# Linear attention and a GELU layer on one core: longer idle products at the start, and another order of chunk 3 and the state products

## The chip, the cores and the metric

The kernel runs on one core of one Trainium2 chip. The metric is the device time of one execution in microseconds (us), as the median of several runs. A profile is one further execution, recorded by the hardware profiler; its span runs from the first to the last instruction.

## The reference

Decayed linear attention over 4 batches, 8 heads, 768 positions and a head size of 64, block by block, and then two matrix products with an exact GELU between them, on all 3072 tokens:

```python
intra = einsum('bhic,bhjc->bhij', qb, kb) * Dmask      # lam ** (i - j) for i >= j, else 0
intra = einsum('bhij,bhjd->bhid', intra, vb)
inter = einsum('bhid,bhde->bhie', qb * lam_pow, kv_state)
out[block] = intra + inter
kv_state = lam_block * kv_state + einsum('bhsd,bhse->bhde', kb * rev_pow, vb)
...
x = out.transpose(0, 2, 1, 3).reshape(3072, 512)
result = gelu(x @ w_in) @ w_out                        # 512 -> 2048 -> 512
```

All inputs and the result are float32 in device memory.

## The kernel before

The kernel works in chunks of 128 positions of one batch, with all heads: 24 chunks, numbered so that four of them (one per batch, the same 128 positions) form a group of 512 tokens. There are six groups. A chunk goes through these steps, each a function of the kernel:

- `transposed`: the matrix engine (TensorE, PE in the profile) transposes keys and queries through PSUM (L169), and another engine copies them out (kT and qT, L172).
- `scores`: products of kT and qT into two PSUM banks (L196); `masked` multiplies them by the decay mask on VectorE (DVE, L204).
- `outputs`: the masked scores times v (L231), for later groups also the queries times the state (L226); the result is copied into x_t (L239 on ScalarE, ACT, for the first groups), the input of the MLP.
- `next_state`: keys times decayed values (v_dec, made by `decay_v`, L163, on GpSimd, POOL) into a PSUM bank with the tag "t", of which there is one (L211). VectorE empties it into the state (L215), which the chunk of the same batch in the next group needs.

The MLP of a group (`mlp_blocks`) is a list of blocks: the first layer, with its GELU on ScalarE (h_ps, L412, into g_t, L416), and the second layer. For group 0 the first layer has 21 blocks, cut so that the first of them need only the first chunks of x_t: blocks 0 to 5 use chunks 0 and 1, blocks 6 and 7 chunk 2, blocks 8 to 13 chunks 0 to 2, blocks 14 to 16 chunk 3, and blocks 17 to 20 all four. The second layer of group 0 is in plain form (L426); later groups use seven products of half blocks in place of eight.

The order of all work is written out by hand. Each engine takes its instructions in the order of the program, and a wait for another engine holds up what stands behind it. Three parts fix the order:

- The opening, straight-line code from `make_powers()` on. `keep_warm(n)` puts n idle products (L470) with a zero operand into PE's stream; `new=False` uses the PSUM bank of the last such run.
- `group0`, a table from the number of a block of group 0 to the steps that are issued just before that block.
- `todo`, a sorted list for all later groups.

Loads are issued by GpSimd in one queue: for chunks 0 to 3 the keys, queries and values with the pieces of w_in between them, then v_dec of chunks 0 to 2, two quarters of w_out, v_dec of chunk 3, two more quarters, and the loads of chunk 4 and so on.

PSUM is tight: the tags "sc", "mh" and "mo" have two banks each, "t" and "o" one. `transposed` takes "mh" for keys and "mo" for queries; each block of the first layer takes "mh"; idle products and the second layer take "mo".

Of the kernel before, what the change touches and what calls it, by code (L numbers as in the profile page):

```python
# [15 lines left out]
def kernel(  # L16
# [123 lines left out]
    def make_lam_blk():  # L140
        for hi in range(2):
            p = slice(hi * D, (hi + 1) * D)
            nc.scalar.copy(lam_blk[p, :, p], lam_c_b[p])
# [7 lines left out]
    def bank(shape, dtype, tag, name):  # L151
        return ps.tile(shape, dtype, tag=tag, name=name, bufs=2 if tag in ("sc", "mh", "mo") else 1)
# [12 lines left out]
    def transposed(c, name, tag, empty):  # L165

        src, t_ps = getattr(c, name), bank([128, HP, C], BF16, tag, "t_ps")
        for hp in range(HP):
            nc.tensor.transpose(t_ps[:, hp, :], src[:, 2 * hp:2 * hp + 2, :], ident)  # L169
        dst = work_pool.tile([128, HP, C], BF16, tag=name + "T", name=name + "T")  # L170
        setattr(c, name + "T", dst)
        empty(dst, t_ps)  # L172
# [18 lines left out]
    def scores(c):  # L191
        sc_ps = [bank([128, HP, C], F32, "sc", f"sc_ps{hi}") for hi in range(2)]
        for hp in range(HP):
            for hi in range(2):
                p = slice(hi * D, (hi + 1) * D)
                nc.tensor.matmul(sc_ps[hi][:, hp, :], c.kT[p, hp, :], c.qT[p, hp, :], start=True, stop=True)  # L196
        c.sc_m = work_pool.tile([128, HP, 2, C], BF16, tag="sc_m", name="sc_m")
        c.sc_ps = sc_ps
        for hi in range(0 if c.n == 0 else 2):
            masked(c, hi)  # L200

    def masked(c, hi):
        mask = decay[:, hi] if c.early else cmask[:, None, :].to_broadcast((128, HP, C))
        nc.vector.tensor_mul(c.sc_m[:, :, hi, :], c.sc_ps[hi], mask)  # L204

    def next_state(c):
        if c.sb == NB - 1:
            return
        kv_ps = bank([128, HP, 128], F32, "t", "kv_ps")
        for hp in range(HP):  # L210
            nc.tensor.matmul(kv_ps[:, hp, :], c.k[:, 2 * hp:2 * hp + 2, :], c.v_dec[:, 2 * hp:2 * hp + 2, :],  # L211
                             start=True, stop=True)
        new = work_pool.tile([128, HP, 128], BF16, tag="state_f", name="state", bufs=8)
        if c.sb == 0:
            nc.vector.tensor_mul(new, kv_ps, lam_blk)  # L215
        else:
            tmp = work_pool.tile([128, HP, 128], F32, tag="tmp", name="tmp")
            nc.vector.tensor_add(tmp, kv_ps, states[c.n])  # L218
            nc.vector.tensor_mul(new, tmp, lam_blk)  # L219
        states[c.n + M] = new  # L220

    def outputs(c, x_t, off, evacuate=True):
        o_ps = bank([128, HP, C], F32, "o", "o_ps")
        if c.sb > 0:
            for hp in range(HP):
                nc.tensor.matmul(o_ps[:, hp, :], states[c.n][:, hp, :], c.qT[:, hp, :],  # L226
                                 start=(hp == 0), stop=False, skip_group_check=True)
        v = c.v if c.early else c.v_dec
        for hi in range(2):
            for hp in range(HP):  # L230
                nc.tensor.matmul(o_ps[hi * D:(hi + 1) * D, hp, :], v[:, 2 * hp + hi, :], c.sc_m[:, hp, hi, :],  # L231
                                 start=(c.sb == 0 and hp == 0), stop=True, skip_group_check=True)
        c.x_o, c.o_ps = x_t[:, :, off * C:(off + 1) * C], o_ps
        if evacuate:
            empty_outputs(c)
# [225 lines left out]
    live = {}  # L461
# [3 lines left out]
    def keep_warm(n, new=True, cols=256):  # L465

        if new:
            idle_ps[0] = bank([128, 512], F32, "mo", "idle_ps")
        for _ in range(n):
            nc.tensor.matmul(idle_ps[0][:, :cols], idle[:, :128], idle[:, :cols], start=True, stop=True)  # L470

    def early(n):
        live[n] = begin(n, early=True)
        return live[n]
# [3 lines left out]
    def causal(hi):  # L478
        nc.vector.tensor_mul(decay[:, hi], decay[:, hi], cmask[:, None, :].to_broadcast((128, HP, C)))

    make_powers()
    nc.scalar.activation(warm, pos, ACT.Gelu)
    keep_warm(8, cols=512)
    c = early(0)
    causal(0)
    transposed(c, "k", "mh", copy)
    keep_warm(1, new=False)
    transposed(c, "q", "mo", copy)
    causal(1)
    keep_warm(1)  # L490
    scores(c)
    for hi in range(2):
        masked(c, hi)
# [6 lines left out]
    nc.scalar.copy(w_in_t[:, :, :256], wide_w)  # L500
    keep_warm(2)
    scores(c)
    keep_warm(8, new=False)
    make_lam_blk()
    outputs(live[1], xT[0], 1)
    c = early(2)
# [34 lines left out]
    def both_transposed(c):  # L541
        transposed(c, "k", "mh", nc.vector.tensor_copy)
        transposed(c, "q", "mo", nc.vector.tensor_copy)
# [2 lines left out]
    group0 = {  # L546
        1: [lambda: scores(live[2])],
        5: [lambda: outputs(live[2], xT[0], 2)],
        9: [lambda: both_transposed(live[3])],
        10: [lambda: scores(live[3]), lambda: next_state(live[0])],  # L550
        11: [lambda: next_state(live[1])],
        12: [lambda: outputs(live[3], xT[0], 3)],
        13: [lambda: next_state(live[2])],
        17: [lambda: next_state(live[3])],
        e: [w_out_sums, lambda: decay_v(live[4], nc.vector)],
        e + 8: [lambda: transposes(live[4])],
# [79 lines left out]
```

## Time and profile before

| | |
|---|---|
| median of 3 runs | 211.65 us (211.26 to 211.77) |
| profiled execution | 211.83 us |
| its span | 210.1 us |
| PE busy | 201.6 us (96%) |
| VectorE busy | 139.1 us (66%) |
| ScalarE busy | 81.6 us (39%) |
| GpSimd busy | 96.0 us (46%) |

Busy times are sums over the whole span. PE's matrix products are pipelined: the length of a row holds the passage through the array, so successive rows overlap, and a row's count times the distance of two starts is the better measure of work. In the rows of the order of time, the first number is the start in us from the beginning of the span, the second the length; "x8" is the number of instructions merged into the row; what stands in brackets is the idle time of the engine just before it and what ended that.

### The profile page before, as it was taken

The numbers are of one execution on the slowest core, as the hardware profiler recorded it, in microseconds if no ns is written. First come the engines' busy times: TensorE is split into PE (matmuls) and PEld (weight loads), VectorE is DVE, ScalarE is ACT, GpSimd is POOL, SyncE is SP. The second block draws the span as 40 slices with busy tenths as digits, with TensorE's granted clock in tenths as the row PEclk, the third lists the DMA queues.
The fourth block names the chain that finished last, engine by engine and source line by source line (L and its number), as shares of the span: only waits on it lengthen the run. The fifth ranks groups of instructions, "written<-read, shape, count | busy, mean of one in ns | idle before, by whom it ended". The sixth has DMA issues, their size and how long they took to land.

```text
span 210.1 us, 4145 instructions
## 1 busy us (share of the span) xinstructions
PE 201.6 (96%) x1718; PEld 131.1 (62%) x1718; DVE 139.1 (66%) x220; ACT 81.6 (39%) x145; POOL 96.0 (46%) x112
## 2 busy tenths in 40 slices
PE   6799799999999999999999999999999999999992
PEld 1567484556544688655688655688655688544881
DVE  4742529455568869698779688579778579223482
ACT  5856264132565420155520255420265420366200
POOL 8999953999999990299500394000100000000000
PEclk9999999999999999999999999999999999999999
DMA  5999999999999999499990599110552000500014
GB/s 117 153 174 177 200 207 186 155 216 151 146 223 144 157 165 98 158 158 150 162 77 0 188 142 172 33 21 3 204 107 41 3 0 3 200 0 0 3 50 150
DMA packets 102370, 24.65 MB, mean 117 GB/s; under 512 B 92880, under 2 KB 99536, under 8 KB 102352
## 3 DMA queue, kind: packets, MB, share of 16 engines
q0 software_dynamic: 80688, 13.37, 88.2%
q1 hardware_dynamic: 21664, 11.02, 23.2%
q8 instruction: 13, 0.21, 0.4%
q14 instruction: 5, 0.04, 0.1%
HBM read 27.27 MB, written 6.29 MB: 160 GB/s over the span
## 4 chain that ended last, share of the span: by engine, by line
PE 92%; DMA 2%; DVE 1%; ACT 1%; POOL 1%; issue 1%; POOLq 0%
PE h_ps L412 40%; PE r_ps L306 9%; PE p_ps L306 8%; PE q_ps L306 8%; PE o_ps L426 7%; PE o_ps L231 4%; PE s_ps L306 4%; PE sc_ps L196 4%; DMA q_t<-in_q_dram 2%; PE o_ps L226 2%; PE kv_ps L211 2%; PE t_ps L169 2%; PE idle_ps L470 1%; ACT g_t L416 1%; POOL k_t L67 0%
## 5 line engine op out<-in xcount | busy, mean ns | idle before, releaser
L412 PE MATMUL h_ps<-x_t,w_in_t 128*128 128x512 bf16 (+3 forms) x460 | 90.0, 344 | 0.6 <-ACT g_t L416 0.2
L416 ACT ACTIVATE g_t<-h_ps 128x512 bf16<-128x512 f32 (+2 forms) x101 | 58.1, 576 | 81.6 <-PE h_ps L412 81.3
L412 PEld LDWEIGHTS <-w_in_t 128*128 128x128 bf16 x460 | 40.1, 98 | 36.6 <-issue 1.5
L163 POOL TENSOR_TENSOR v_dec<-v_t,lam_m 128x512 bf16<-128x512 bf16 x23 | 24.5, 1079 | 48.1 <-PE kv_ps L211 47.0
L306 PEld LDWEIGHTS <-g_sum 128*128 128x128 bf16 x400 | 38.5, 98 | 5.1
L281 DVE TENSOR_TENSOR g_sum<-g_t 128x1024 bf16<-128x1024 bf16 x50 | 33.4, 716 | 10.7 <-ACT g_t L416 10.7
L204 DVE TENSOR_TENSOR sc_m<-sc_ps,cmask 128x512 bf16<-128x512 f32 x40 | 25.6, 682 | 2.0 <-PE sc_ps L196 2.0
L67 POOL DMA_DIRECT2D k_t<-in_k_dram x24 | 22.1, 922 | 2.2 <-DMA w_out_t<-in_moe_w_out_dram 2.0
L67 POOL DMA_DIRECT2D q_t<-in_q_dram x24 | 21.5, 898 | 2.3 <-DMA w_out_t<-in_moe_w_out_dram 2.3
L67 POOL DMA_DIRECT2D v_t<-in_v_dram x24 | 21.4, 893 | 2.0 <-DMA w_out_t<-in_moe_w_out_dram 1.7
L306 PE MATMUL r_ps<-w_sum,g_sum 128*128 128x256 bf16 x160 | 19.3, 273 | 0.0
L241 DVE TENSOR_TENSOR x_t<-o_ps,lam_q 128x512 bf16<-128x512 f32 x16 | 11.0, 688 | 10.2 <-PE o_ps L231 10.2
L306 PEld LDWEIGHTS <-g_t 128*128 128x128 bf16 x160 | 15.3, 98 | 3.2
L218 DVE TENSOR_TENSOR tmp<-kv_ps,state 128x512 f32<-128x512 f32 x16 | 11.0, 690 | 7.4 <-PE kv_ps L211 7.4
L426 PE MATMUL o_ps<-w_out_t,g_t 128*128 128x512 bf16 x64 | 15.3, 380 | 0.0
L219 DVE TENSOR_TENSOR state<-tmp,lam_blk 128x512 bf16<-128x512 f32 x16 | 14.8, 923 | 0.5
L196 PE MATMUL sc_ps<-qT,kT 64*128 64x128 bf16 x192 | 10.0, 226 | 0.3 <-DVE qT L172 0.3
L306 PE MATMUL p_ps<-w_sum,g_t 128*128 128x256 bf16 x80 | 10.1, 273 | 0.0
L306 PE MATMUL q_ps<-w_sum,g_t 128*128 128x256 bf16 x80 | 9.7, 273 | 0.0
L426 PEld LDWEIGHTS <-g_t 128*128 128x128 bf16 x64 | 5.8, 98 | 6.1
L306 PE MATMUL q_ps<-w_out_t,g_sum 128*128 128x256 bf16 x80 | 9.6, 273 | 0.0
L306 PE MATMUL s_ps<-w_sum,g_sum 128*128 128x256 bf16 x80 | 9.6, 273 | 0.0
(65 smaller groups left out, 168.1 us busy)
## 6 DMA issues: line engine op xcount, KB each, us to landing
out_dram<-o_sb SPq DMA_DIRECT2D x9, 512.0 KB, 3.0
k_t<-in_k_dram POOLq DMA_DIRECT2D x24, 128.0 KB, 6.0
q_t<-in_q_dram POOLq DMA_DIRECT2D x24, 128.0 KB, 6.2
v_t<-in_v_dram POOLq DMA_DIRECT2D x24, 128.0 KB, 6.5
w_out_t<-in_moe_w_out_dram POOLq DMA_DIRECT2D x4, 512.0 KB, 10.4
w_in_t<-in_moe_w_in_dram POOLq DMA_DIRECT2D x7, 256.0 KB, 7.9
out_dram<-o_sb SPq DMA_DIRECT2D x5, 256.0 KB, 5.2
wide_w<-in_moe_w_in_dram SPq DMA_DIRECT2D x1, 512.0 KB, 4.1
```

Of the source, the lines that this page charges most:

```text
L67: nc.gpsimd.dma_start(raw[n, name], chunk_of(name, n))
L163: eng.tensor_mul(c.v_dec, c.v, lam_m[:, :, None].to_broadcast((128, H, D)))
L196: nc.tensor.matmul(sc_ps[hi][:, hp, :], c.kT[p, hp, :], c.qT[p, hp, :], start=True, stop=True)
L204: nc.vector.tensor_mul(c.sc_m[:, :, hi, :], c.sc_ps[hi], mask)
L218: nc.vector.tensor_add(tmp, kv_ps, states[c.n])
L219: nc.vector.tensor_mul(new, tmp, lam_blk)
L241: nc.vector.tensor_mul(c.x_o, c.o_ps, lam_q)
L281: nc.vector.tensor_tensor(gsum[i][:, ks, :], g_t[:, ka + k:ka + k + n4, ta], g_t[:, kb + k:kb + k + n4, tb], op=op)
L306: nc.tensor.matmul(o, left[i](k, slice(u * C, (u + 1) * C)), right[i](k), start=(begin and k == 0), stop=(k == KH - 1), skip_group_check=True)
L412: nc.tensor.matmul(h_ps[:, k, lo:hi], w_in_t[:, ki, (kf + k) * 128:(kf + k + 1) * 128], x_t[:, ki, cols.start + lo:cols.start + hi], start ...
L416: nc.scalar.activation(g_t[:, kf:kf + ks, cols], h_ps, ACT.Gelu)
L426: nc.tensor.matmul(om[io], g_t[:, kf, io * C:(io + 1) * C], w_out_t[:, kf, :], start=(kf == 0), stop=(kf == NK2 - 1))
```

## The change

In the opening, the first run of idle products goes from eight to eleven of 512 columns; behind the transposes of chunk 0's keys stand three idle products of 256 columns in place of one, behind those of its queries two in place of one, and before the outputs of chunk 1 nine in place of eight.

In the table for group 0, the state products of chunks 0, 1 and 2 move from ahead of blocks 10, 11 and 13 to ahead of blocks 6, 7 and 9. The transposes of chunk 3 move from ahead of block 9 to ahead of block 8. The scores of chunk 3 stay ahead of block 10, its outputs ahead of block 12, and the state product of chunk 3 ahead of block 17.

```diff
     make_powers()
     nc.scalar.activation(warm, pos, ACT.Gelu)
-    keep_warm(8, cols=512)
+    keep_warm(11, cols=512)
     c = early(0)
     causal(0)
     transposed(c, "k", "mh", copy)
-    keep_warm(1, new=False)
+    keep_warm(3, new=False)
     transposed(c, "q", "mo", copy)
     causal(1)
-    keep_warm(1)
+    keep_warm(2)
     scores(c)
...
     scores(c)
-    keep_warm(8, new=False)
+    keep_warm(9, new=False)
     make_lam_blk()
     outputs(live[1], xT[0], 1)
...
     group0 = {
         1: [lambda: scores(live[2])],
         5: [lambda: outputs(live[2], xT[0], 2)],
-        9: [lambda: both_transposed(live[3])],
-        10: [lambda: scores(live[3]), lambda: next_state(live[0])],
-        11: [lambda: next_state(live[1])],
+        6: [lambda: next_state(live[0])],
+        7: [lambda: next_state(live[1])],
+        8: [lambda: both_transposed(live[3])],
+        9: [lambda: next_state(live[2])],
+        10: [lambda: scores(live[3])],
         12: [lambda: outputs(live[3], xT[0], 3)],
-        13: [lambda: next_state(live[2])],
         17: [lambda: next_state(live[3])],
```

## The prediction

> **What bounds the kernel now.** I read the page's head first, then the waits of the matmul engine (PE), then the order of time, for PE and for the engines that feed it.
>
> ```profile
> span 210.1 us, 4145 instructions
> ...
> PE 201.6 (96%) x1718; PEld 131.1 (62%) x1718; DVE 139.1 (66%) x220; ACT 81.6 (39%) x145; POOL 96.0 (46%) x112
> ```
> ```profile
> PE t_ps L169 <- DMA k_t<-in_k_dram: 1.3, 1, 1.3
> ...
> PE kv_ps L211 <- DVE state L215: 1.0, 1, 1.0
> ...
> PE h_ps L412 <- ACT g_t L416: 0.2, 1, 0.2
> PE h_ps L412 <- ACT x_t L239: 0.2, 1, 0.2
> ```
>
> PE is busy for 96% of the span, and the second fence holds the waits of PE that matter (two of 0.3 stand in the rows below). So PE's own stream sets the end, and whatever moves the stream forward early moves the end, unless a transfer is late afterwards. But a busy PE is not one at full speed, which the opening shows in the order of time (start, length, what; x is a count):
>
> ```profile
> 1.19 3.59 PE L470 MATMUL idle_ps<-idle 128*128 128x512 bf16 x8 [1.19 <-DVE idle L101]
> ...
> 2.02 0.15 PEld L470 LDWEIGHTS <-idle 128*128 128x128 bf16 x1 [0.28 <-issue]
> ...
> 3.73 0.15 PEld L470 LDWEIGHTS <-idle 128*128 128x128 bf16 x1 [0.28 <-issue]
> ...
> 6.12 0.61 PE L169 MATMUL t_ps<-ident,k_t 128*128 128x128 bf16 x4 [1.34 <-DMA k_t<-in_k_dram]
> 6.53 0.42 PE L470 MATMUL idle_ps<-idle 128*128 128x256 bf16 x1
> 7.22 0.61 PE L169 MATMUL t_ps<-ident,q_t 128*128 128x128 bf16 x4 [0.27 <-DMA q_t<-in_q_dram]
> ...
> 8.34 0.61 PE L196 MATMUL sc_ps<-qT,kT 64*128 64x128 bf16 x8 [0.30 <-DVE qT L172]
> ...
> 10.35 0.63 PE L169 MATMUL t_ps<-ident,q_t 128*128 128x128 bf16 x4
> ...
> 12.58 1.29 PE L470 MATMUL idle_ps<-idle 128*128 128x256 bf16 x8
> ...
> 14.34 0.40 PE L169 MATMUL t_ps<-ident,k_t 128*128 128x128 bf16 x4
> ...
> 15.07 0.60 PE L412 MATMUL h_ps<-x_t,w_in_t 128*128 128x256 bf16 x4
> ```
>
> Four transposes take 0.61 to 0.63 us up to 10.35 and 0.40 at 14.34. Eight idle products of 256 columns fit into 1.29 us at 12.58, where the single one at 6.53 took 0.42. So PE ran at half rate until about 13.1, inside the idle run at 12.58. The first idle run of 3.59 us did not raise the rate; unbroken work from 8.34 to 13.1, 4.8 us, did. In between lie the waits of 1.34, 0.27 and 0.30.
>
> The second place is the stage of chunk 3 and the state products:
>
> ```profile
> 17.22 3.13 POOL L163 TENSOR_TENSOR v_dec<-v_t,lam_m 128x512 bf16<-128x512 bf16 x3
> ...
> 18.34 0.61 PE L412 MATMUL h_ps<-x_t,w_in_t 128*128 128x256 bf16 x4
> 18.46 0.59 ACT L239 CAST x_t<-o_ps 128x512 bf16<-128x512 f32 x1
> ...
> 19.10 1.50 PE L412 MATMUL h_ps<-x_t,w_in_t 128*128 128x128 bf16 x24 [0.15 <-ACT x_t L239]
> ...
> 20.19 0.87 ACT L416 ACTIVATE g_t<-h_ps 128x512 bf16<-128x512 f32 x2 [0.82 <-PE h_ps L412]
> ...
> 20.84 0.81 PE L412 MATMUL h_ps<-x_t,w_in_t 128*128 128x384 bf16 x4 [0.24 <-ACT g_t L416]
> 21.48 0.39 PE L169 MATMUL t_ps<-ident,k_t 128*128 128x128 bf16 x4
> ...
> 22.25 0.41 DVE L172 COPY qT<-t_ps 128x512 bf16<-128x512 bf16 x1
> 22.97 0.40 PE L196 MATMUL sc_ps<-qT,kT 64*128 64x128 bf16 x8
> 23.30 0.40 PE L211 MATMUL kv_ps<-v_dec,k_t 128*128 128x128 bf16 x4
> 23.40 1.29 DVE L204 TENSOR_TENSOR sc_m<-sc_ps,decay 128x512 bf16<-128x512 f32 x2 [0.73 <-PE sc_ps L196]
> 23.53 0.81 PE L412 MATMUL h_ps<-x_t,w_in_t 128*128 128x384 bf16 x4
> 24.61 0.68 DVE L215 TENSOR_TENSOR state<-kv_ps,lam_blk 128x512 bf16<-128x512 f32 x1
> 25.34 0.40 PE L211 MATMUL kv_ps<-v_dec,k_t 128*128 128x128 bf16 x4 [1.00 <-DVE state L215]
> 26.32 0.42 PE L231 MATMUL o_ps<-sc_m,v_t 128*64 128x128 bf16 x8
> 26.68 0.82 PE L412 MATMUL h_ps<-x_t,w_in_t 128*128 128x384 bf16 x4
> ```
>
> The state product of chunk 1 (25.34) waits 1.00 us for its PSUM bank, tag "t", of which there is one. The vector engine empties it at 24.61, only after both masks of chunk 3 (23.40, 1.29 us). Two more waits fall on the activation engine: 0.24 us before block 8 for the Gelu of block 6, and 0.15 before block 6 for chunk 2's outputs.
>
> I count what PE issues by start to start, since lengths hold a tail of about 0.17 us. From the rows: a block of 4x384 is 0.64 (20.84 to 21.48), of 4x256 0.44 (0.61 less the tail), of 16x128 0.89 and of 8x128 0.45 (1.50 less 0.16, over 24); a state product 0.23, scores 0.33, outputs 0.36, one chunk's two transposes 0.45 (from 0.39 and a tail each).
>
> **Part 1: the idle products.** The start-to-start of the idle products is (3.73 - 2.02)/4 = 0.43 us. Eleven run to 1.19 + 11 x 0.43 = 5.9, with the tail 6.1: just up to the first keys at 6.12, whose transposes they don't delay. Should the keys land earlier, at most 0.43 us of a product lies ahead of them. The two added behind the keys' transposes make three, 0.21 apart from 6.53, so until 7.17: again just up to 7.22. The one behind the queries' fills a wait that ends at 8.34. The ninth before chunk 1's outputs costs 0.11 at full rate, and is hidden while the masks of chunk 1 run (1.29 us). So these five cost nothing in place, and at most 0.1 if the masks were no cover.
>
> What they bring is the rate. By the trace, 3.59 us of work was too little and 4.8 enough; work from 1.19 without a break reaches 4.8 us at 6.0, so I take full rate from about 6.1. If it came only at 8, the sum below would be the same, for the reason that now follows: it isn't PE alone that limits the opening.
>
> ```profile
> 12.68 1.29 DVE L204 TENSOR_TENSOR sc_m<-sc_ps,decay 128x512 bf16<-128x512 f32 x2 [1.23 <-PE sc_ps L196]
> ...
> 14.44 0.59 ACT L239 CAST x_t<-o_ps 128x512 bf16<-128x512 f32 x1 [0.58 <-PE o_ps L231]
> ```
> ```profile
> L67 POOL DMA_DIRECT2D q_t<-in_q_dram x1: 939/939/939, 8.4 to 8.4; - x1
> ...
> DMA to landing us min/median/max: 5.6/5.6/5.6
> ```
>
> Put chunk 1's query transposes no sooner than today, 10.35. At full rate they end at 10.74 and their copy at 11.2; scores to 11.65; masks to 13.0; outputs to 13.4; the copy to x_t (0.59) ends at 14.0, where today it ends at 15.03. But ahead of block 0 stand chunk 2's transposes, and its queries land at 8.4 + 5.6 = 14.0 whatever PE does. Four transposes (0.22) and one idle product (0.11) later block 0 starts at 14.35. Today it starts behind x_t, at 15.07. So the opening gives 0.7 us and no more: the next that is late is a transfer.
>
> The Trainium skill ("TensorE: Matmul & The Clock Gate", Part 1) says that full clock follows one busy window of about 3.4 us whose phase runs free of the kernel. The trace agrees as far as 3.59 us were not enough and 4.8 were. By a strict reading (a window wholly busy) the run of 4.7 us would hold one in (4.7 - 3.4)/3.4 = 38% of phases only, an estimate from that page; the time would then be that of rival A below.
>
> **Part 2: the order of the state products.** Shifted by 0.7, block 5 starts at 17.62 and issues until 18.06; x_t of chunk 2 is ready at 19.05 - 0.72 = 18.33. Now the state product of chunk 0 stands first, and it needs the decayed values of chunk 0, which the POOL engine makes as the first of three from 17.22, 1.04 us each: 18.3, 19.3, 20.35. POOL's queue doesn't move with PE. So:
> The state product of chunk 0 starts at 18.40 and block 6 at 18.62; the wait for x_t, 18.33, is covered by it. Block 6 issues until 19.51. The vector engine empties the bank from 18.83 to 19.52, with nothing else queued, so chunk 1's product starts at 19.57 (bound: 0.06 here, up to 0.3 if POOL's and the vector engine's work, side by side here for the first time, slow each other by a fifth; I take 0.06, from the lengths in the rows). Block 7 issues 19.80 to 20.24. Then chunk 3's transposes ask for a bank of tag "mh" and wait for the Gelu of block 6 (0.61, done about 20.33): 20.37 to 20.82. Block 8 waits for block 7's Gelu until 20.86, then issues to 21.50. Chunk 2's product, 0.23, has its bank (emptied by 20.7). Block 9 to 22.38. Scores of chunk 3: the queries' copy follows at 21.15 to 21.55, so nothing waits; 22.38 to 22.71. Blocks 10 and 11 until 24.0. The masks run from 22.82 to 24.11, behind chunk 2's state (to 22.63), so chunk 3's outputs stall for at most 0.1; they issue 24.01 to 24.37. Block 12 starts at 24.37 and not at 26.68, which is 2.31, and the state product that followed it is already done, 0.22 more: **2.53 us**.
>
> Of these the opening is worth less than its 0.7, as POOL holds the first state product until 18.4: with the opening as it is today I find 2.0 (rival A). The order takes away the 1.00 and the smaller waits, and covers two that remain. Nothing more than about 0.24 of waiting is left in that stretch, so a gain over 2.8 is excluded.
>
> **What could be late next.** The waits of PE in the second fence all lie before 27. The next fixed times are transfers:
>
> ```profile
> 34.57 7.07 PE L426 MATMUL o_ps<-w_out_t,g_t 128*128 128x512 bf16 x32
> ```
> ```profile
> L92 POOL DMA_DIRECT2D w_out_t<-in_moe_w_out_dram x1: 757/757/757, 23.5 to 23.5; - x1
> ...
> DMA to landing us min/median/max: 12.5/12.5/12.5
> ```
>
> The last quarter of w_out lands at 23.5 + 12.5 = 36.0. Its first use is six blocks of 0.87 into the second layer, 34.57 + 5.2 = 39.8 today and 37.2 afterwards: 1.2 us are left. So I cost this at nothing, and the whole lead reaches the end.
>
> **The sum.** The profiled execution took 211.83 us, 1.7 around its span, and 0.18 above the median of 211.65. Against its own time: 211.83 - 2.53 = 209.3; against the median 209.1. I say 209.2.
>
> **Rivals.** *A, the clock does not come earlier*: the short break at 6.06, or those near 8.1, count like the 1.34 did. Then block 0 starts at 15.07, or 15.17 behind the ninth idle product, and the state product of chunk 0 fits into the wait before block 6 at 19.16. From there all is as above, 0.54 later: a gain of 2.0, 209.8. For it: the waits of 0.27 and 0.30 kept the rate down before. Against it: the 4.8 us without any. Chance 0.13.
>
> *B, slower: the clock falls back.* With the opening faster than its transfers, PE waits for about 1.2 of the 1.8 us before 14.35. If that drops the rate and, as from 8.34, it takes 4.8 us of unbroken work to come back, the loss is half of that, 2.4: break-even, 211.7. If the breaks between 18 and 21 hold it down for a second stretch, 4.8 are lost: 214.1. It decides from 6.3 us at half rate on. Against it: the wait of 1.00 at 25.34 left the block at 26.68 at 0.82, as at 20.84. Chance 0.03.
>
> *C, a transfer takes the lead back*, leaving under 0.3%: the last quarter of w_out would have to land over 3 us later than today (1.2 of margin and 1.9 of the lead), because PE's earlier reads and writes disturb it. About 211.4. For it: 12.5 us from issue to landing show a full queue. Against it: that queue is filled by POOL, whose order and times the change leaves alone. Chance 0.04.
>
> **How the numbers follow.** The forecast has 0.80. Its own range is a gain of 2.2 to 2.8 with 0.25 of scatter (the three runs lie 0.51 apart), 208.7 to 209.7; with rival A the range ends at 210.0. A difference of 0.3% (0.6 us) is about what can be told from none. Forecast and A are faster: 0.93; C is the same, 0.04; B slower, 0.03.
>
> **What would show it.** Right: four transposes at 0.39 to 0.40 by 7.2; block 0 near 14.35, released by the transposes of chunk 2 and its queries' landing; the state product of chunk 0 near 18.4 released by POOL; no wait of PE for the state over 0.1; block 12 near 24.4; the second layer at about 32.0 and no wait for w_out. Wrong: idle products of 256 columns still 0.2 apart at 10 (A), blocks of 4x256 at 0.87 after 14.35 (B), or a wait of PE for w_out or for chunk 4's loads (C).

## The result, and the profile after

The changed kernel takes 209.91 us, the median of four runs (209.78 to 210.04), against 211.70 before: a ratio of 0.992 with a 95% interval of 0.9903 to 0.9937, 1.8 us less. The forecast was 209.2, with 208.7 to 209.7 as its own range and an upper end of 210.0 for rival A. The direction was right. The time lies above the forecast's own range, and only the part that was added for A, which did not happen, holds it; the gain is 0.7 of what the sum said. The profiled execution took 209.99 us.

The head of its page, and all waits of PE that it lists (those over 0.15 us) but the very first, for the zero operand:

```profile
span 208.2 us, 4142 instructions
...
PE 200.3 (96%) x1708; PEld 130.5 (63%) x1725; DVE 139.0 (67%) x220; ACT 81.7 (39%) x145; POOL 97.1 (47%) x112
```
```profile
PE t_ps L169 <- DMA q_t<-in_q_dram: 0.7, 2, 0.4
PE t_ps L169 <- DMA k_t<-in_k_dram: 0.6, 1, 0.6
PE sc_ps L196 <- DVE qT L172: 0.3, 1, 0.3
```

The wait of 1.00 for the state's bank is gone, and so are those of 0.24 and 0.15 for the activation engine. In their place stand waits of the opening for transfers. The order of time on PE:

```profile
1.19 4.87 PE L470 MATMUL idle_ps<-idle 128*128 128x512 bf16 x11 [1.19 <-DVE idle L101]
6.16 0.40 PE L169 MATMUL t_ps<-ident,k_t 128*128 128x128 bf16 x4
...
13.42 0.40 PE L169 MATMUL t_ps<-ident,k_t 128*128 128x128 bf16 x4 [0.56 <-DMA k_t<-in_k_dram]
14.25 0.40 PE L169 MATMUL t_ps<-ident,q_t 128*128 128x128 bf16 x4 [0.44 <-DMA q_t<-in_q_dram]
...
14.60 0.60 PE L412 MATMUL h_ps<-x_t,w_in_t 128*128 128x256 bf16 x4
...
17.90 0.61 PE L412 MATMUL h_ps<-x_t,w_in_t 128*128 128x256 bf16 x4
18.57 0.38 PE L211 MATMUL kv_ps<-v_dec,k_t 128*128 128x128 bf16 x4
18.79 1.06 PE L412 MATMUL h_ps<-x_t,w_in_t 128*128 128x128 bf16 x16
19.81 0.40 PE L211 MATMUL kv_ps<-v_dec,k_t 128*128 128x128 bf16 x4
...
21.12 0.81 PE L412 MATMUL h_ps<-x_t,w_in_t 128*128 128x384 bf16 x4
...
21.99 0.81 PE L412 MATMUL h_ps<-x_t,w_in_t 128*128 128x384 bf16 x4
22.74 0.40 PE L196 MATMUL sc_ps<-qT,kT 64*128 64x128 bf16 x8
...
24.47 0.42 PE L231 MATMUL o_ps<-sc_m,v_t 128*64 128x128 bf16 x8
24.83 4.24 PE L412 MATMUL h_ps<-x_t,w_in_t 128*128 128x384 bf16 x56
...
32.58 7.07 PE L426 MATMUL o_ps<-w_out_t,g_t 128*128 128x512 bf16 x32
```

The transposes take 0.40 from 6.16 on: in this execution full rate came with the eleven idle products. Block 0 starts at 14.60 behind the landing of chunk 2's queries, block 12 at 24.83 (24.37 was forecast), the second layer at 32.58, which is 1.99 us sooner than before. The rows of the first two state products (18.57 and 19.81) show no wait, since a wait that is shorter than the tail of the row before it is not listed. Block 5 has issued by 18.34 (17.90 + 0.44), so the first state product starts 0.23 later than it could; it follows the end of POOL's first product at 18.5, the first of the three in this row:

```profile
17.46 3.05 POOL L163 TENSOR_TENSOR v_dec<-v_t,lam_m 128x512 bf16<-128x512 bf16 x3
```

### The profile page after: what moved, and what is told of

Read it like the earlier page. It is cut to its first block, busy times and chain, and to the rows that moved or that the text cites. A ratio compares the mean times of both kernels' runs of the same rounds, so it can differ in the third digit from the quotient of the medians.

```text
span 208.2 us, 4142 instructions
## 1 busy us (share of the span) xinstructions
PE 200.3 (96%) x1708; PEld 130.5 (63%) x1725; DVE 139.0 (67%) x220; ACT 81.7 (39%) x145; POOL 97.1 (47%) x112
## 4 chain that ended last, share of the span: by engine, by line
PE 86%; POOL 8%; DVE 3%; issue 1%; POOLq 0%; DVEq 0%
PE h_ps L412 39%; PE p_ps L306 9%; PE r_ps L306 8%; PE q_ps L306 8%; PE o_ps L426 7%; PE o_ps L231 4%; PE s_ps L306 3%; PE sc_ps L196 3%; PE kv_ps L211 3%; POOL w_in_t L88 3%; PE o_ps L226 2%; POOL k_t L67 2%; POOL q_t L67 2%; POOL v_t L67 2%; PE t_ps L169 1%
## 5 line engine op out<-in xcount | busy, mean ns | idle before, releaser
L412 PE MATMUL h_ps<-x_t,w_in_t 128*128 128x512 bf16 (+3 forms) x446 | 88.7, 343 | 0.6
L163 POOL TENSOR_TENSOR v_dec<-v_t,lam_m 128x512 bf16<-128x512 bf16 x23 | 25.2, 1101 | 44.5 <-PE kv_ps L211 42.9
L281 DVE TENSOR_TENSOR g_sum<-g_t 128x1024 bf16<-128x1024 bf16 x50 | 33.6, 716 | 11.3 <-ACT g_t L416 11.3
L426 PE MATMUL o_ps<-w_out_t,g_t 128*128 128x512 bf16 x61 | 14.8, 380 | 0.1
L196 PE MATMUL sc_ps<-qT,kT 64*128 64x128 bf16 x192 | 9.5, 218 | 0.3 <-DVE qT L172 0.3
L470 PE MATMUL idle_ps<-idle 128*128 128x256 bf16 (+1 forms) x33 | 8.4, 393 | 1.2 <-DVE idle L101 1.2
L306 PE MATMUL p_ps<-w_out_t,g_sum 128*128 128x256 bf16 x80 | 9.6, 273 | 0.0
```

The costliest lines, as they stand in the source:

```text
L163: eng.tensor_mul(c.v_dec, c.v, lam_m[:, :, None].to_broadcast((128, H, D)))
L281: nc.vector.tensor_tensor(gsum[i][:, ks, :], g_t[:, ka + k:ka + k + n4, ta], g_t[:, kb + k:kb + k + n4, tb], op=op)
L306: nc.tensor.matmul(o, left[i](k, slice(u * C, (u + 1) * C)), right[i](k), start=(begin and k == 0), stop=(k == KH - 1), skip_group_check=True)
L412: nc.tensor.matmul(h_ps[:, k, lo:hi], w_in_t[:, ki, (kf + k) * 128:(kf + k + 1) * 128], x_t[:, ki, cols.start + lo:cols.start + hi], start ...
L426: nc.tensor.matmul(om[io], g_t[:, kf, io * C:(io + 1) * C], w_out_t[:, kf, :], start=(kf == 0), stop=(kf == NK2 - 1))
```

## The experiments

Three more series of runs were made, each with its own runs of the kernel before, whose medians were 212.51 (e1 to e4), 211.53 (e5 to e8) and 211.91 (e9 to e12). The first of the three ran on another chip than the other two. The kernel before scatters more from execution to execution than its first three runs showed, by up to 2.2 us in one series. So times are compared within a series, and starts in the traces beside them. By the times alone the size of the gain is not settled: it is 0.8% in the first four runs and in e8, and 1.3% for e3 and e4, which differ from the changed kernel by one small edit each. What follows on sizes goes by the traces.

**The two parts alone.** e1 has the new idle products and the old table for group 0, e2 the reverse.

> The longer idle products with the old order of chunk 3 and the state products. Theory (the opening is ahead by 0.47 us at block 0, held there by the landing of chunk 2's queries, and in the old order no state product asks for POOL's result before 22.8, so nothing takes the 0.47 back): full rate from about 6, block 0 at 14.6, the wait of 1.00 for the state bank still there at about 24.9, second layer at 34.1, 0.45 us faster than before: about 211.2. Rival (the rate in the opening is worth nothing, since transfers set it): 211.65. Rival (the new opening is most of the gain of 1.8): 210.3.

> The new order of chunk 3 and the state products with the old idle products. Theory: half rate until 9.5 or later, block 0 at 15.07, the first state product at 18.8 inside the wait for chunk 2's outputs, block 6 at 19.10 (0.31 later than with both parts), no wait for the state bank over 0.15, second layer at 32.9, a gain of 1.5 to 1.7: 210.0 to 210.2. So the parts add up to more (2.1) than both together (1.8), because POOL's first product holds what the opening wins. Rival (the opening carries half of the gain): 210.8.

e1: 211.32 us, a ratio of 0.9957 (0.9929 to 0.9986); expected were 0.45 us, 0.2%, which the interval holds. e2: 210.10, 0.989 (0.9866 to 0.9915); the time is as expected, the gain in this series is larger than the 1.5 to 1.7 us. In e1's trace block 0 starts at 13.91, since chunk 2's queries landed sooner, at 13.5; that lead of 1.16 went through to 1.07 at the end of the span, and the wait for the state's bank is still there. In this order the first state product comes at 22.23, and POOL made its operand by 18.4, so POOL takes nothing back:

```profile
13.57 0.40 PE L169 MATMUL t_ps<-ident,q_t 128*128 128x128 bf16 x4 [0.42 <-DMA q_t<-in_q_dram]
...
13.91 0.60 PE L412 MATMUL h_ps<-x_t,w_in_t 128*128 128x256 bf16 x4
...
24.28 0.40 PE L211 MATMUL kv_ps<-v_dec,k_t 128*128 128x128 bf16 x4 [1.00 <-DVE state L215]
```

In e2's trace the second layer starts at 33.26, 1.31 before the old time, although block 0 starts 0.46 later (15.53: chunk 0's queries landed at 7.6): 1.77 for the order alone, where 1.5 to 1.7 was expected. So the order is the larger part, and e1 gives the opening a part of its own. That the parts add up to more than the whole (0.43% and 1.1%, against 1.3% for e3 and e4 beside them, which have all or nearly all of both) fits the theory, but the intervals overlap.

**Fewer idle products.**

> The changed kernel with 8 instead of 11 products in the first idle run, the other idle products as in the change. Theory (an early full rate needs work without a break of over a microsecond): half rate until 9.5 or later, block 0 at 15.0 to 15.1, block 6 about 0.3 later than with the change, 210.2. Rival (the products between the transposes are what brings the rate): full rate by 9, 209.9.

```diff
-    keep_warm(11, cols=512)
+    keep_warm(8, cols=512)
```

209.70 us (209.69 to 209.99): my expectation missed, and the rival's too, since the rate was up before the products between the transposes ran:

```profile
1.20 3.60 PE L470 MATMUL idle_ps<-idle 128*128 128x512 bf16 x8 [1.20 <-DVE idle L101]
6.12 0.40 PE L169 MATMUL t_ps<-ident,k_t 128*128 128x128 bf16 x4 [1.33 <-DMA k_t<-in_k_dram]
```

The same eight products, the same wait of 1.33, but here full rate at 6.12, where the kernel before had 0.61. It differs from execution to execution, then. Of the executions profiled with eight products two came to full rate at 13.1 and 13.3, three at 4.2 to 5.3, of which two lost it again (e11 and e12); all nine with eleven came to it by 7.1, of which one lost it again (e8). These times are those of the clock record of the traces.

**The kernel before again.**

> The kernel before once more, for a second profile. Theory: the landing of chunk 0's queries and the arrival of the full rate differ from execution to execution and show in block 0's start and the end alike; the full rate comes either before 6 or after 11.5, as the eight products fill a window of 3.4 us or not. Rival (fixed to the program): 13.1 again.

211.61 us, and a second form of its opening (window, then busy time of the engines, the granted clock ahead of the last two columns):

```profile
5.00:10.00 5.00, 3.03 (x28) 2.12 (x29) 3.94 (x8) 4.93 (x13) 5.00 (x7) 0.76 2.38 154
10.00:15.00 5.00, 4.93 (x60) 3.34 (x58) 2.70 (x6) 2.96 (x7) 5.00 (x8) 0.90 1.94 174
```

The granted clock is the mean of 1 at full and 0.5 at half rate, so half rate held for 0.24 x 2 of the first 5 us and for 0.10 x 2 of the next, 3.4 us together: the rate was up at 4.2, fell back at 7.6 and returned at 11.0. The rival's 13.1 did not come again, and the loss of a rate that was already up is a form that I had not expected. Block 0 started at 14.26, and the end lay 0.8 sooner than in the first profile, as block 0 did.

**The gate.** If POOL's first product sets the start of the stage, an earlier opening is worth nothing, and an earlier product is. e5 loads chunk 2's keys and queries ahead of a piece of w_in; e6 lets POOL make v_dec of chunks 0 and 1 ahead of the last two pieces of w_in; e7 does both; e8 is the changed kernel in the same series.

```diff
# e5
-    for item in "k0 q0 v0 k1 q1 v1 w1 k2 q2 v2 ...
+    for item in "k0 q0 v0 k1 q1 v1 k2 q2 w1 v2 ...
# e6, behind the nine idle products; w6 and w7 are taken out of the list above
+    for n in range(2):
+        decay_v(live[n], nc.gpsimd)
+    load_w_in(12, 2)
+    load_w_in(14, 2)
```

> The changed kernel with the keys and queries of chunk 2 loaded ahead of the second piece of w_in instead of behind it. Theory (POOL's first product at about 18.45 holds what the opening wins): the queries of chunk 2 land at about 12.8, block 0 starts near 13.6 instead of 14.1 to 14.6, but the first state product still starts at 18.5 to 18.7, released by POOL, and the time stays within 0.1 of the changed kernel's. Rival (the landing of chunk 2's queries is what limits the whole): 0.5 to 1.0 lower.

> The changed kernel with the decayed values of chunks 0 and 1 made by POOL ahead of the last two pieces of w_in, so 1.5 us sooner. Theory: no wait for POOL before the first state product; block 6 then follows chunk 2's outputs directly, 0.1 to 0.5 us sooner by the landing of chunk 2's queries in the execution, and the scatter of the opening shows in the time again: 209.3 to 209.8, runs apart by more than with the changed kernel. Rival (POOL does not hold anything): no difference.

> Both of the last two edits. Theory: block 0 near 13.6, the first state product near 17.9 without a wait for POOL, a new wait of up to 0.4 for the third piece of w_in (lands at 16.4) before block 4, and the time 0.5 to 0.7 under the changed kernel's: about 209.1. Rival (another gate follows at once, such as the bank of the state products or the Gelus): as the changed kernel, 209.7.

> The changed kernel once more, on the chip of the last three. Theory (POOL's product is the gate, so the scatter of transfers and clock in the opening does not reach the end): 209.7 to 210.0, and its runs lie within 0.35 of each other while those of the kernel before lie over 1.0 apart if the chip is one that scatters. Rival (the scatter before has another cause): both scatter alike.

e5, waits of PE and its order of time:

```profile
PE kv_ps L211 <- POOL v_dec L163: 1.0, 1, 1.0
```
```profile
13.60 0.60 PE L412 MATMUL h_ps<-x_t,w_in_t 128*128 128x256 bf16 x4
...
18.45 0.38 PE L211 MATMUL kv_ps<-v_dec,k_t 128*128 128x128 bf16 x4 [0.97 <-POOL v_dec L163]
```

Block 0 starts a whole microsecond sooner than after the change, and all of it comes back as a wait of 0.97 for POOL; the time, 209.99, is that of the changed kernel beside it, 209.96. e6, order of time on PE and POOL:

```profile
13.93 0.60 PE L412 MATMUL h_ps<-x_t,w_in_t 128*128 128x256 bf16 x4
...
15.73 2.17 POOL L163 TENSOR_TENSOR v_dec<-v_t,lam_m 128x512 bf16<-128x512 bf16 x2
...
17.78 0.39 PE L211 MATMUL kv_ps<-v_dec,k_t 128*128 128x128 bf16 x4
```

The first state product starts at 17.78 without a wait, right behind block 5 (17.33 + 0.44), and the span ends at 207.3 instead of 208.2 and 208.3 (this profile is of the fastest of e6's six runs). It isn't the opening that brings this: in e3, a run told further below that leaves these two products of POOL where they were, block 0 starts at 14.06, only 0.13 later than in e6, but the first state product 0.67 later:

```profile
18.45 0.38 PE L211 MATMUL kv_ps<-v_dec,k_t 128*128 128x128 bf16 x4 [0.47 <-POOL v_dec L163]
```

So the gate is shown, from both sides. The median is 209.39 (209.05 to 210.45); e7's is 209.42 (208.85 to 210.35), no better than e6, where 209.1 was expected: in its profile chunk 0's queries landed at 7.7 and took the rest back. Both lie about 0.5 us below the changed kernel, but their ratios to the kernel before (0.9909 and 0.9905, against 0.9924) have overlapping intervals: the times suggest the gain and don't show it. Without the gate more scatter was expected, and e6's runs lie 1.40 apart and e7's 1.50; but e5's, with the gate, lie 1.14 apart. e8's six runs lie 0.68 apart (209.69 to 210.37), the eleven of the kernel before 1.03: not the 0.35 that I had expected, so the times don't show that the gate holds the scatter back. One profile shows what can move a run:

```profile
6.37 0.49 PE L470 MATMUL idle_ps<-idle 128*128 128x256 bf16 x3
8.02 0.61 PE L169 MATMUL t_ps<-ident,q_t 128*128 128x128 bf16 x4 [1.16 <-DMA q_t<-in_q_dram]
```
```profile
5.00:10.00 5.00, 3.04 (x25) 1.70 (x24) 2.65 (x6) 4.82 (x13) 5.00 (x7) 0.80 2.29 148
10.00:15.00 5.00, 5.00 (x57) 3.69 (x56) 3.27 (x7) 2.75 (x5) 5.00 (x8) 0.86 1.97 175
```

Chunk 0's queries landed 0.9 late, and the rate fell back from 8.0 to 11.4. Block 0 started at 15.13, 0.53 later than in the first profile, and the first state product at 18.84, 0.27 later: the time that PE had spent waiting for POOL there takes up about half.

e12 is e6 with the old idle products.

> New order with POOL's first two products sooner (as in e6), but the old idle products. Theory (without POOL's gate the opening's lead counts): 0.4 to 1.0 slower than e6, 209.8 to 210.4, where with the gate the idle products were worth 0 to 0.3. Rival (idle products worth nothing in this order either way): as e6, 209.4.

209.78 (209.48 to 210.49), 0.9916 (0.9886 to 0.9947): 0.4 above e6, in another series and within the scatter. In its profile chunk 0's queries landed late (7.8), the rate was lost from 7.8 to 11.3, block 0 started at 14.95, and the first state product starts at 18.66 with no wait for POOL. By the ratios (0.9909 and 0.9916) the two can't be told apart: what the new idle products are worth without the gate isn't settled.

**The step between product shapes.** In the rows after the change, block 9 issues from 21.99 for 0.64 and the scores start at 22.74, 0.1 late, although the copy of their queries had ended at 21.70; the outputs at 24.47 are 0.1 late likewise. At the outputs a second cause falls on the same moment, since the second mask of chunk 3 ended only at 24.46:

```profile
23.17 1.29 DVE L204 TENSOR_TENSOR sc_m<-sc_ps,decay 128x512 bf16<-128x512 f32 x2 [0.28 <-PE sc_ps L196]
```

That row alone can't tell a step from a stall. In the kernel before, the masks had ended at 24.69 (23.40 + 1.29), and the outputs were late by the same 0.1 (26.23 to 26.32). e9 and e10 add one product ahead of each first-layer block of groups 1 to 5, 80 in all, with 64 or 128 rows of weights:

```diff
+                if g > 0:
+                    nc.tensor.matmul(h_ps[:, 0, :128], idle[:64, :128], idle[:64, :128], start=True, stop=True, ...)
```

> The changed kernel with one more idle product ahead of each first-layer block of groups 1 to 5 (80 in all), 128 columns, with 64 rows of weights; it leaves the result alone, since the block's first product overwrites it. Theory (a step from a 128x128 product to a 64-row one costs PE about 0.096 us on entering and 0.1 on leaving, no matter what else waits): 80 x (0.056 + 0.2) = 20 us over the changed kernel, 230. Rival 1 (only entering costs): 12 us over, 222. Rival 2 (what I took for it is a wait for the copies of the queries): as with 128 rows, 4.5 us over, 214.4.

> The same with 128 rows of weights. All theories: 80 x 0.056 = 4.5 us over the changed kernel, 214.4.

229.02 and 214.21 us, where the theory had 230 and 214.4 and the rivals 222 or 214.4 for e9. They are 14.8 apart, 0.185 for each product. e9, then e10:

```profile
64.95 1.04 PE L415 MATMUL h_ps<-x_t,w_in_t 128*128 128x512 bf16 x4
65.92 0.23 PE L409 MATMUL h_ps<-idle 64*128 64x128 bf16 x1
66.08 1.04 PE L415 MATMUL h_ps<-x_t,w_in_t 128*128 128x512 bf16 x4
```
```profile
63.29 1.03 PE L415 MATMUL h_ps<-x_t,w_in_t 128*128 128x512 bf16 x4
64.15 0.22 PE L409 MATMUL h_ps<-idle 128*128 128x128 bf16 x1
64.21 1.03 PE L415 MATMUL h_ps<-x_t,w_in_t 128*128 128x512 bf16 x4
```

Start to start the block is 0.97 against 0.86, the added product 0.16 against 0.06: 0.1 on entering a 64-row product and 0.1 on leaving it. That is the shape of the scores. The outputs are products of 128 rows and 64 columns, which no run was made for: their 0.1 rests on the rows of the kernel before.

**The late loss.** In the first profile after the change the lead shrinks from 1.98 to 1.81 at 83 us. VectorE's and POOL's order of time:

```profile
77.48 1.40 DVE L281 TENSOR_TENSOR g_sum<-g_t 128x1024 bf16<-128x1024 bf16 x1
```
```profile
77.26 1.06 POOL L163 TENSOR_TENSOR v_dec<-v_t,lam_m 128x512 bf16<-128x512 bf16 x1
```

A sum that otherwise takes 0.69 took 1.40 beside POOL's product, which had begun 0.22 before it; it ended 0.56 after that product did. VectorE's queue behind it was 0.7 late, and PE waited for it once, at 83.12. e3 moves that product of POOL behind the next loads.

> The changed kernel, with the decayed values of chunk 14 made by POOL behind the loads of chunk 17 instead of ahead of them. Theory (of the lead of 1.98 us, 0.17 is lost at 83 us because a sum of two halves of g on VectorE took 1.40 us beside POOL's product, and PE waits for the queue behind it): that sum takes 0.69 again, the products at line 306 follow without a wait, the lead stays 1.98 beyond 85 us, and the time is 0.15 to 0.2 lower than with the change: 209.7. Rival (the 0.17 has another cause, such as the transfers at that time): the lead falls to 1.81 again, 209.9.

e3 took 209.71 (209.70 to 209.74), the sum 0.69, and its lead is 2.10 on both sides of that place. But e4 and e8, without the edit, keep their lead there too, with sums of 0.81 and 0.69 at that place. e12, which has POOL's product in the old place here, shows the loss again: its lead falls from 1.89 to 1.71.

```profile
77.58 1.41 DVE L281 TENSOR_TENSOR g_sum<-g_t 128x1024 bf16<-128x1024 bf16 x1
```
```profile
77.37 1.06 POOL L163 TENSOR_TENSOR v_dec<-v_t,lam_m 128x512 bf16<-128x512 bf16 x1
```

So two executions lose 0.17 and 0.18, both with the long sum at this place; its cause is read from the rows, and that e3's edit is what removed it is not shown.

## Why the prediction came out as it did

**What held.** PE's stream set the end; the order took away the wait of 1.00 and the smaller ones; chunk 2's queries gated block 0 (14.60, forecast 14.35: they landed at 14.2, not 14.0); POOL gated the first state product (18.57, forecast 18.40, and e5, e3 and e6 bear out the gate); w_out was no gate although its last quarter landed at 36.9, 0.8 later than before.

**What failed is the sum of part 2**, 2.53, which measured 2.07 (26.68 - 24.83 + 0.22). Term by term: POOL's products began 0.24 later (17.46, not 17.22), and with them the first state product 0.17 later than the forecast had it; I had taken their start from one execution as fixed, and in e11, the kernel before again, it is 17.52. The state's bank took 1.24 from one product to the next, not 1.17, and block 8 another 0.02; and two times 0.10 are the gaps ahead of the scores and the outputs, the largest of the four. These I had read in the trace before (22.88 to 22.97, and 26.23 to 26.32) as waits that the new order would take away. They cost the same before and after; e9 and e10 measure such a step for products of the scores' shape. At the outputs the stall of "at most 0.1" for the mask, which I had named and put at nothing, would have come to about the same, since the mask ended at 24.46. Together 0.46, which is the difference.

**Two losses behind it** that I had put at nothing. Blocks 12 to 16 issue without chunk 2's state product between them, so that block 14, which needs block 12's bank, waits 0.09 at 26.23 for block 12's Gelu: two blocks issue in 1.30, while that Gelu starts 0.86 after its block and takes 0.49, until 26.18. The 0.22 of that product had been the cover. And 0.17 went at 83 us in this execution. 2.53 - 0.46 - 0.09 - 0.17 = 1.81, and the two profiled executions differ by 1.84. The path and the waits were right, then. Wrong were the sizes of terms, each taken too favourably, and above all two costs that I took for waits.

**What was luck.** The time lies below 210.0 and near rival A's 209.8, but A's cause is not what brought it there. And the rate came at 5.9, where I had 6.1 but by a rule that the runs refute (the next paragraph tells how): in the nine profiles with eleven products it came between 4.1 and 7.0.

**The rivals.** A, a clock that doesn't come earlier, was not seen in any of nine profiles with eleven products. "3.59 us were too little and 4.8 enough", as I had it, is refuted: in e4, e11 and e12 the eight products, 3.35 to 3.60 us long, were enough. By the Trainium skill ("TensorE: Matmul & The Clock Gate", Part 1) the rate is decided in windows of 3.4 us of free phase. The traces agree with the length: the rate lost in e8, e11 and e12 was lost for 3.4 us each. The free phase would explain why eleven products brought an early rate in nine profiles of nine and eight in three of five; no run here set the phase, so this is not shown. My strict reading, that only wholly busy windows count (38%), did not hold: in e4 the eight products had ended (4.8) 0.5 us before the rate rose (5.3 in the clock record). B, a clock that falls back in the opening's waits, did happen, in e8. I had priced it at 2.4 us, to break-even. Together with queries that landed 0.9 late it cost 0.3 at the first state product: the fall lasted from 8.0 to 11.4, while transfers set the pace, and was over before the first block. C did not happen.

## What to carry to other kernels

A lead won in one stage is worth what the next gate leaves of it: list, for every engine that the stage after will ask, the time at which its result is fixed anyway, and change that first (here the place of two POOL products in a queue of loads: about 0.7 us at the first state product). Before a gap is booked as a wait that can go, look for the semaphore that ends it; a gap with none, of the same size at every place with the same two product shapes, is a cost and stays. And where one execution's profile carries the forecast, take the landing of the first transfers and the clock's phase as things that change from one execution to the next.

## What the runs showed that I had not expected

A 64-row product between 128x128 ones costs PE 0.1 us on entering and 0.1 on leaving: 80 of them took 14.8 us more than 80 of 128 rows. The kernel before runs in 210.8 to 213.1 us, on two chips, without any change to it. In its two profiles block 0 starts 0.81 apart and the end lies 0.8 apart, so there the opening's landings and clock reach the end; the slowest runs have no profile.

And a bf16 sum of two tiles on VectorE can take 1.40 us instead of 0.69. In the two rows above it began about 0.2 after a product of POOL and ended 0.56 after it. But in the first profile after the change a sum that began at the same time as such a product, at 69.36, took 0.68, and POOL's product 1.59 instead of 1.06; and in e4 a sum at 71.55 took 1.52 with no product of POOL beside it. The rows suggest that the two engines' work delays each other, but what makes a sum long is not settled here.
